# A pooled-attention and token-mixing kernel on one core: the written issue order drawn up anew, with each weight block's signs right behind its absolute values

## The chip, the cores and the metric

The kernel runs on one core of one Trainium2 chip. The time is device time in microseconds (us). It was taken three times for the kernel before: 647.41, 647.52 and 649.43, median 647.52. A core has TensorE (PE in the rows, its weight loads are PEld), VectorE (DVE), ScalarE (ACT) and GpSimd (POOL), which compute, and SyncE (SP), which here issues nearly all DMA transfers. Each engine takes its own instructions strictly in the order in which the program issues them.

## The reference

Inputs are q, k, v of 8 batches, 8 heads, 576 tokens and 64 channels, and four weight matrices. The weights arrive as 64-bit floats.

```
k_p, v_p = mean of k, v over groups of 8 tokens          # 72 keys per head
attn     = softmax(q @ k_p.T / sqrt(64)); sum gets +1e-9 # per head, 576 x 72
x        = attn @ v_p, heads side by side                # 8 x 576 x 512
theta    = x @ w_theta                                   # 512 x 512
zr, zi   = x * cos(theta), x * sin(theta)
y        = w_tok_r @ zr + w_tok_i @ zi                   # contraction over tokens, 576 x 576 each
u        = x + y
out      = u + max(u @ w_ch, 0)                          # 512 x 512
```

## The kernel before

The work is cut into named streams, each a Python generator whose every step issues a few instructions. A stream's name tells its batch and its part: k (load keys), K (pool them, turn them into `kpT`), Q (load and turn queries), v and V (the same for values), S (softmax of one tile of 128 tokens), E (turn the attention by 16 small DMAs, batches 2 to 7 only), X (attention times values, one pair of heads, into `xT`), T (rotate: theta, sine, cosine, z of one tile), Z (split a quarter of z in two parts, zh and zl), M (mix: the token contraction for one quarter of the channels and one part of the tokens), F (final: w_ch, relu, output). Without a batch: h0 to h3 (w_theta by 128 rows), w0.0 to w4.0 (the token matrices by 128 rows, .0 real and .1 imaginary), W0 to W4 (their transposition on PE), c0 to c3 (w_ch).

Products that need more than PE's short format are done in three matmuls: each operand is split in a high part (a cast) and a low part (the rest), which is what the names ending in h and l are. M has 27 matmuls for each of its 64 pieces: zh with WTh, zh with WTl, zl with WTh (the order is reversed for the second token part).

What sets the order is a table, the string `SCHEDULE` at line 30: 1834 words, each the name of a stream. A word issues that stream's next step. A last letter v, g or a tells the engine of a step that has a choice: DVE, POOL or ACT. The loop at the end of `tile_attn_moe` reads it:

```
for word in SCHEDULE.split():
    name, engine = (word[:-1], word[-1]) if word[-1] in "vga" else (word, None)
    now[0] = engine
    next(streams[name])
```

There is no other planner: semaphores between engines follow from the data. A buffer's next user waits until its last one is done.

The steps that the prediction speaks of, by line:

- `to_f32` makes 32-bit floats of 64-bit ones, for each block of h, w and c. Its five steps: the absolute value of the high words on ACT (L289), the sign bits of the same words on ACT, written as 16-bit halves of a block that is otherwise zero (L293), both joined on DVE (L300), the power of two on DVE (L302), the low words times that power on DVE (L304). Only the two ACT steps are free of each other. The sign blocks are two buffers, `chh_st` and `chl_st`, used in turn.
- `token_weights` (L345) loads a w block and calls `to_f32`; `turn_weights` (L373) transposes it on PE (L377, L380) and splits it (L172 high part, L388 low part).
- `load` (L441 to L456) loads keys and values; `pool_on_pe` (L497, L499) sums groups of 8 on PE for batch 0; `keys` (L508, L518) transposes the sums. The second half of the keys of batch 0, k0.1, goes into the buffer `early`. For batch 1 the groups are summed by `pool_sum` (L423, L428) on DVE or POOL.
- `soften`: scores on PE (L637), their maximum on DVE (L667), the exponentials with their sums on ACT (L672, eight of L675, L691, in batches 0 and 1), the reciprocal (L695) and the products (L714, L721). In batch 0, tiles 1 and 3 use a buffer named `spare`.
- `rotate`: the low part xl (L851), the matmuls for theta (L858, bank pt), rounding on ACT (L862), the difference on DVE (L864), sine and cosine on ACT (L875, L878, L883).
- `take`: zh (L172) and zl (L909). `mix`: py (L923), u (L929), uh (L172), ul (L936). `final`: pf (L952), oT (L958).

```
nc.scalar.activation(t, hi.bitcast(F32), AF.Abs, scale=2.0**-112)      # L289
yield
nc.scalar.activation(sign..., hi.bitcast(F32), AF.Copy, scale=2.0**-60) # L293
yield
nc.vector.scalar_tensor_tensor(ti, ti, 3, sign, ...)                    # L300
```

Of the kernel before, what the change touches and what calls it, by code (L numbers as in the profile page):

```python
# [30 lines left out]
k0.1 k0.0 Q0.0 w0.0 w0.0 w0.0 K0.0 K0.0a K0.1 w0.0 k0.2 h0 Q0.4 h0 h0 h0 K0.1a K0 Q0.0 Q0.0v h0 h1 h1 K0.2 K0.2v  # L31
Q0.1 h0 h1 h1 h0 h1 K0a K0 K0v S0.0 S0.0 h2 h2 h2 h2 h0v h0 Q0.4 Q0.4v Q0.1 Q0.1a Q0.3 Q0.3 Q0.3v S0.1 S0.0 S0.0
S0.0 S0.1 S0.1 S0.1 S0.1 Q0.2 Q0.2 h1 Q0.2v S0.2 S0.0 S0.0v S0.0g w0.1 w1.0 w0.1 w0.1 w1.0 h2 h2 k1.0 w0.0 w0.0
S0.2 S0.2 S0.2 S0.2 w0.1 K1.0v S0.1 w1.0 w1.0 v0.0 S0.3 S0.3 S0.3 S0.0 w1.0 w1.0 S0.1g S0.1v v0.1 V0.0 V0.1 V0v
S0.3 v0.2 V0.2 S0.4 S0.2 V0 S0.4 S0.1 S0.0v S0.1a S0.0 S0.0a h1 h1v h1 k1.1 K1.1g w1.1 h2 h3 h3 h3 h3 w0.1 h3 h3
w0.1 S0.1 S0.1a S0.2g S0.2g S0.2 S0.2a X0.0.0 X0.0.0a K1 S0.3 S0.3 S0.3g S0.2 S0.2v X0.0.1 X0.0.1v S0.4 S0.4
S0.4 w1.1 h2a Q1.0 h3 Q1.0 h3a X0.0.3 S0.3g S0.3 S0.3a S0.3 S0.4 S0.4g S0.3v k1.2 K1.2g X0.0.3v W0 W0a S0.4g
X0.0.2 K1v h2 X0.0.2v T0.0g T0.0g S0.4 W0 S0.4a S0.4 S0.4a X0.2.2 X0.2.2a w2.1 T0.1a w2.0 w2.0 W0 W0a w2.1 h3
w1.1 w1.1 v1.0 V1.0v w1.1 w1.1 W0 T0.0 T0.0 X0.2.0 X0.2.0a T0.0 T0.0 T0.0 W1 v1.2 W1a X0.2.1 X0.2.1a T0.0a T0.0
X0.2.3 w4.0 w2.1 w2.1 w3.0 w2.0 w2.0 w2.0 w2.1 w2.0 T0.1v T0.1 X0.2.3a X0.2.3a T0.2g w2.1 T0.1 W1 W1 T0.0 K1  # L40
T0.0 W1v W1 T0.4a w3.0 w3.0 T0.1 T0.1 T0.1 T0.1a K1v Q1.1 Q1.1 W2 W2a w3.0 w3.0 w3.0 W2 w3.1 T0.2g T0.2 T0.4g
T0.1 T0.2 T0.2 T0.2 T0.2 T0.2a T0.2 T0.1 T0.3g T0.3g T0.3 T0.2 T0.1 T0.3 T0.2 T0.3 W2 W2a W2 T0.4 w3.1 w3.1 w3.1
w3.1 w3.1 w4.0 w4.0 w4.0 w4.0 W3 T0.3 T0.3 T0.4 T0.4 T0.4 W3a T0.4 v1.1 V1.1g V1g c0 W3 T0.3a T0.3 T0.3 T0.3 c0
c0 w4.0 W3 W3a W3 T0.4 T0.4 Z0.0a V1.2g c0 c0 c0 Z0.0v W4 c0v W4a W4 W4a W4 W4v W4 Z0.1a Z0.1v W4a W4 k2.2 K2.2v
M0.0.0 M0.0.0 c0g c0g c1 c1 c1 c1 c1 c1 c1v c1v c1v M0.0.1 Z0.2g S1.0 c2 c2 M0.0.0v M0.0.0g c2 M0.0.1 M0.0.1g
S1.0 S1.0 Z0.2v M0.1.0 M0.1.0 c2 c2 c2 c2v c2g M0.2.0 V1g M0.2.0 M0.2.0a M0.2.0g S1.0 M0.1.0a S1.0v S1.0v c2v V1
V1g c3 c3 c3 M0.1.1 Z0.3v M0.1.1 M0.1.1a M0.1.1g S1.0 S1.0a S1.1 S1.1 S1.1 S1.0 S1.0 S1.0v S1.0 S1.1 S1.1v
M0.2.1 M0.2.1 Z0.3g S1.1g M0.3.0 c3 c3 V1v M0.2.1a M0.2.1v S1.1 c3 c3g c3g c3g S1.2 S1.2 S1.2 S1.1v S1.1 S1.1
M0.3.0 S1.2 Q2.0 S1.1a M0.3.0g M0.3.0g S1.1 M0.3.1 M0.3.1 S1.3 S1.3 X1.0.0 X1.0.0v S1.2g S1.2g M0.3.1v M0.0.1v
v2.2 M0.1.0g k2.0 K2.0g S1.3 F0.0.0 F0.0.0 F0.0.0 X1.0.1 X1.0.1a M0.3.1v F0.0.1 F0.0.1 F0.0.1 S1.4 S1.4 X1.0.2  # L50
X1.0.2v Q2.0 S1.3 F0.1.0 F0.1.0 X1.0.3 X1.0.3a T1.0g T1.1a S1.2 S1.2a S1.2 S1.2 S1.2a S1.2 F0.1.1 F0.1.1 S1.3g
S1.3g F0.0.1 S1.3 S1.3v k2.1 S1.3 S1.3 S1.3v S1.3 F0.1.0 F0.1.1 T1.0g K2.1g T1.0 S1.4 S1.4 T1.0 T1.0 T1.0 T1.0
T1.0a T1.0 F0.2.1 F0.2.1 S1.4g S1.4g S1.4 S1.4v S1.4 S1.4 S1.4v S1.4 T1.0 T1.0 T1.1g T1.1 X1.2.0 X1.2.0a Q2.1
Q2.1 K2 K2a V2.2g v2.0 k3.2 X1.2.1 T1.1 T1.1 K2 K2a S2.0 S2.0 X1.2.1a V2.0g X1.2.2 X1.2.2a X1.2.3 X1.2.3v T1.2v
T1.2v v2.1 V2.1g T1.3g T1.3g T1.1 T1.1 T1.1a F0.1.1 T1.1 T1.1 S2.0 T1.1 S2.0 S2.0g T1.2 T1.2 T1.2 F0.2.0 F0.2.0
F0.2.0 K3.2g S2.1 S2.1 F0.2.1 T1.2 T1.2 T1.2a T1.2 T1.2 T1.2 k3.0 K3.0g T1.3 S2.1 T1.3 S2.0 S2.1 T1.3 T1.3 Q3.0
X1.2.3a S2.2 T1.4a T1.4g S2.1v S2.1 F0.2.1 S2.2 T1.3 T1.3a T1.3 F0.3.0 S2.2 T1.3 T1.3 T1.4 T1.4 S2.2 T1.4 T1.4
T1.4 T1.4 S2.2v V2g V2g V2 k3.1 K3.1g S2.3 S2.3 T1.4 K3 Z1.0g F0.3.1 V2g V2g F0.3.0 F0.3.0 S2.4 K3a F0.3.1
F0.3.1 Z1.0v M1.0.0 Q3.0 Z1.1a Z1.1v E2.0 S2.2 E2.0a E2.0a M1.0.0 E2.0g E2.0v S2.3 S2.3 S2.3v K3 K3a M1.0.1
M1.0.1 Z1.2a v3.0 V3.0g X2.0.0 X2.0.0v M1.1.0 M1.1.0 S2.3 X2.0.2 X2.0.2a M1.0.0v Z1.2g M1.1.0g Q3.1 M1.2.0 S2.4  # L60
S2.4 M1.1.0g Q3.1 S2.4 S2.4v S2.4 X2.0.1 X2.0.1a M1.2.0 M1.2.0v M1.2.0v v3.1 M1.1.1 M1.1.1 M1.1.1v X2.0.3 V3.1g
v3.2 X2.0.3v T2.0a V3.2g T2.1a S3.0 S3.0 S3.0 k4.0 K4.0g S3.0 Z1.3g M1.0.1g S3.0v T2.0v M1.2.1 M1.2.1 M1.2.1g
Z1.3v M1.1.1g S3.1 M1.0.1g T2.0 S3.1 S3.1 S3.1 M1.3.0 M1.3.0 E2.2 S3.0 E2.2a F0.3.1 E2.2g E2.2g E2.2v T2.0 T2.0
M1.3.1 M1.3.1 M1.3.1a M1.3.1v M1.3.0g M1.3.0g S3.1v M1.2.1g S3.1 X2.2.0 X2.2.0a S3.2 S3.2 X2.2.1 T2.0 T2.0
X2.2.1a T2.0a T2.0 T2.0 T2.0 F1.0.1 X2.2.2 F1.0.1 T2.1v X2.2.2a M1.0.0g F1.0.0 F1.0.0 F1.0.1 k4.1 K4.1g F1.0.0
S3.2 X2.2.3 S3.2 S3.2v X2.2.3a Q4.0 T2.2g X2.2.3a T2.1 F1.0.1 T2.1 T2.1 F1.1.1 S3.3 S3.3 T2.1 T2.1 T2.1a T2.1
T2.1 v4.0 T2.1 V3g V3g T2.2g V3 T2.2 T2.2 T2.2 T2.2 T2.2 F1.1.0 k4.2 T2.2v T2.2 T2.2 T2.3g T2.2 T2.3g T2.3 S3.4
F1.1.1 F1.1.0 F1.1.0 F1.1.1 T2.3 T2.3 V4.0g T2.3 T2.3 T2.3v K4 T2.3 T2.3 T2.3 Q4.0 V3v T2.4g T2.4g K4.2g T2.4
T2.4 T2.4 E3.0 T2.4 E3.0a S3.2 K4a F1.2.0 F1.2.0 T2.4 T2.4 F1.1.1 T2.4 F1.2.1 F1.2.1 E3.0g F1.2.0 F1.2.1 Z2.0a
K4 V3g F1.3.1 F1.3.1 F1.3.0 F1.3.0 Z2.0v Z2.1a Z2.1v E3.0g E3.0g X3.0.0 X3.0.0a S3.3 S3.3 v4.1 V4.1g S3.3g S3.3  # L70
M2.0.0 M2.0.0 Q4.1 M2.0.0g M2.0.0g F1.2.1 S3.4 Q4.1 v4.2 V4.2g S3.4 S3.4 S3.4g X3.0.1 M2.0.1 M2.0.1 S3.4 k5.2
K5.2g M2.1.0 M2.1.0 X3.0.1a X3.0.2 X3.0.2a K4a S4.0 S4.0 S4.0 F1.3.1 F1.3.0 X3.0.3 Z2.2a Z2.2v M2.0.1a M2.0.1g
M2.1.1 M2.1.1 M2.1.1g M2.1.1g X3.0.3a T3.0v T3.0v Z2.3a M2.2.0 M2.1.0g M2.1.0g M2.2.0 M2.2.0a Z2.3v M2.3.0 k5.0
K5.0v M2.3.0 M2.3.0a S4.0 S4.0v E3.2 S4.0 E3.2v E3.2g E3.2g E3.2g M2.2.1 M2.2.1 S4.1 S4.1 S4.1 S4.1 S4.1v M2.3.1
M2.3.1 M2.3.1a M2.3.1v k5.1 K5.1g F1.3.1 S4.2 S4.2 v5.0 T3.0 T3.0 X3.2.0 T3.0 T3.0 X3.2.0a S4.2 M2.2.0g M2.2.1g
M2.2.1v M2.3.0g F2.0.0 S4.1 Q5.0 X3.2.1 X3.2.1v T3.0 T3.0a F2.0.0 F2.0.0 T3.1a T3.1g F2.0.1 F2.0.1 F2.0.1 X3.2.2
X3.2.2a S4.2 S4.2g S4.3 S4.3 X3.2.3 V4g X3.2.3a X3.2.3g T3.1 F2.0.1 S4.4 T3.0 T3.0 T3.0 V4v V4 V4g V4v S4.3
T3.2v T3.2g T3.1 T3.1 F2.1.0 T3.3g S4.3 F2.1.0 F2.1.0 Q5.0 T3.1 T3.1 T3.1a T3.1 T3.3g T3.1 F2.1.1 F2.1.1 T3.1
F2.1.1 E4.0 T3.2 T3.2 T3.2 F2.2.1 F2.2.1 T3.2 T3.2 T3.2v T3.2 T3.2 T3.2 S4.2 T3.3 S4.3v F2.1.1 T3.3 T3.3 K5 K5a
S4.4 T3.3 T3.3 T3.3a T3.3 T3.3 T3.3 F2.2.0 F2.2.0 F2.2.0 F2.2.1 Q5.1 F2.2.1 T3.4g T3.4g T3.4 T3.4 T3.4 T3.4 T3.4  # L80
T3.4 E4.0g Q5.1 T3.4 F2.3.1 F2.3.1 E4.0g E4.0g E4.0g X4.0.0 F2.3.0 K5 K5a F2.3.0 S5.0 V5.0g X4.0.0a S4.3 X4.0.1
X4.0.1a F2.3.0 F2.3.1 Z3.0g Z3.0v M3.0.0 Z3.1v Z3.1v M3.0.0 S4.4 S4.4 S4.4v S4.4 X4.0.2 X4.0.2a M3.0.1 X4.0.3
X4.0.3a M3.0.0a M3.0.1 M3.0.1a M3.0.1g Z3.2a v5.1 V5.1v M3.1.0 T4.1g T4.1v T4.0v T4.0v M3.1.0 M3.1.0a S5.0
M3.1.0g Z3.2v S5.0 S5.0 S5.0v M3.1.1 M3.1.1 M3.2.0 M3.2.0 M3.2.0g Z3.3a Z3.3v M3.3.0 Q6.0 E4.2 E4.2a E4.2v E4.2v
M3.3.0 M3.3.0v E4.2g M3.3.0g S5.1 S5.1 M3.2.1 S5.1 S5.1 X4.2.2 X4.2.2a M3.2.1 M3.2.1v T4.0 S5.0 M3.0.0g X4.2.0
M3.2.0g k6.0 K6.0g F2.3.1 F3.0.0 F3.0.0 F3.0.0 T4.0 T4.0 X4.2.0a v5.2 V5.2g S5.1g S5.1 X4.2.1 X4.2.1a M3.3.1
M3.1.1g M3.1.1v T4.0 T4.0 T4.0v T4.0 k6.1 K6.1g M3.3.1 M3.3.1a T4.0 T4.0 X4.2.3 M3.2.1g X4.2.3v X4.2.3g V5v V5v
V5 V5v V5v M3.3.1g T4.1 T4.1 T4.1 T4.1 T4.1 T4.1a T4.1 T4.1 T4.1 v6.0 T4.2g S5.2 S5.2 F3.0.1 F3.0.1 E5.0 T4.2g
T4.2 F3.1.0 T4.4a T4.2 T4.2 T4.3a T4.3v S5.3 S5.2 S5.2 S5.2g F3.2.0 F3.1.0 F3.0.1 F3.0.1 S5.3 T4.2 T4.2 T4.2a
T4.2 E5.0g E5.0a T4.2 T4.2 T4.3 T4.3 T4.3 F3.1.1 F3.1.0 F3.1.1 F3.1.1 F3.1.1 S5.4 T4.3 F3.2.0 T4.3 T4.3a T4.3  # L90
T4.3 T4.3 T4.4g S5.2 T4.4 T4.4 T4.4 T4.4 T4.4 k6.2 T4.4 T4.4 E5.0g E5.0g F3.2.1 F3.2.1 F3.2.0 F3.2.1 F3.3.1
F3.3.1 V6.0g Z4.0g Z4.0g F3.3.0 F3.3.0 v6.1 S5.3 S5.3 K6.2g V6.1g F3.2.1 Q6.0 F3.3.1 F3.3.0 X5.0.0 X5.0.0v
M4.0.0 M4.0.0 Z4.1a Z4.1g S5.3v S5.3 M4.0.1 X5.0.1 X5.0.1v M4.0.1 M4.1.0 M4.0.0g M4.0.1v M4.0.1g S5.4 S5.4
# [1003 lines left out]
```

## Time and profile before

| what | value |
|---|---|
| three timed runs | 647.41, 647.52, 649.43 us |
| the profiled execution, by its own clock | 646.99 us |
| its span, first to last instruction | 645.1 us |
| mean granted TensorE clock | 0.973 of full speed |
| PE busy | 603.7 us, 94% of the span |
| first scores (L637) | at 16.76 us |
| first theta matmul (L858) | at 57.07 us |
| first mixing matmul (L923) | at 100.2 us |

Positions are us from the start of the span. The profiled execution took 1.89 us more than its span, and is 0.53 under the median of the three runs. "Waits" are times in which an engine had an instruction that could not start; what ended the wait is named behind the arrow. A granted clock of 1.00 is the upper of TensorE's two levels (2.4 GHz); a mean below that mixes the two levels, the lower being 1.2 GHz.

### The profile page before, as it was taken

What the parts mean: (1) busy time and instruction counts of PE and PEld (TensorE: products, weight loads), DVE (VectorE), ACT (ScalarE), POOL (GpSimd) and SP (SyncE); (2) the same over time, 40 slices, a digit from 0 to 9 for tenths busy, and PEclk for the clock granted to TensorE, in tenths of its full rate; (3) what the DMA queues carried; (4) which work ended last, traced back from release to release, by engine and by line L of the source; (5) the groups of instructions that cost most, each with busy time, mean ns of one, the idle gap of its engine ahead of it and who ended that gap; (6) DMA issues with size and microseconds to landing.
All of it is one profiled execution on the core that took longest, in us unless ns stands there. A gap on an engine that the chain in (4) does not pass through costs nothing.

```text
span 645.1 us, 11179 instructions
## 1 busy us (share of the span) xinstructions
PE 603.7 (94%) x4012; PEld 552.0 (86%) x4012; DVE 472.6 (73%) x839; ACT 306.0 (47%) x668; POOL 344.7 (53%) x381
## 2 busy tenths in 40 slices
PE   5878888999879999999999999999999999999996
PEld 4755578987769988999899989998899889999996
DVE  4866589877788877788889877777777787656234
ACT  4847573847872375326542473237522552243010
POOL 2123242557677777675733848774736645451640
PEclk9869698999999999999999999999999999999998
DMA  9859312145764766356566336454252432302204
GB/s 271 217 120 211 83 34 75 35 95 112 134 121 102 123 99 115 78 105 96 88 94 117 76 50 116 95 102 67 45 93 36 81 50 38 60 2 38 38 1 74
DMA packets 239911, 57.83 MB, mean 90 GB/s; under 512 B 227952, under 2 KB 228464, under 8 KB 239856
## 3 DMA queue, kind: packets, MB, share of 16 engines
q1 hardware_dynamic: 239856, 57.12, 45.6%
q8 instruction: 32, 0.52, 0.4%
q14 instruction: 23, 0.19, 0.1%
HBM read 37.81 MB, written 9.44 MB: 73 GB/s over the span
## 4 chain that ended last, share of the span: by engine, by line
PE 60%; DVE 13%; ACT 10%; DMA 5%; POOL 4%; SPq 4%; issue 3%; DVEq 0%; ACTq 0%; POOLq 0%
PE py L923 27%; PE pf L952 10%; PE pt L858 9%; PE pv L835 5%; PE s L637 4%; SPq L788 3%; ACT e L675 2%; DMA kpst<-in_k_dram 2%; DMA vpst<-in_v_dram 1%; PE px L868 1%; DMA wraw<-in_moe_w_tok_r_dram 1%; DVE g L864 1%; ACT g L862 1%; DVE zl L909 1%; PE ths L331 1%
## 5 line engine op out<-in xcount | busy, mean ns | idle before, releaser
L923 PE MATMUL py<-WTl,zh 128*128 128x256 f32 (+1 forms) x576 | 87.3, 296 | 0.0
L923 PE MATMUL py<-WTh,zh 128*128 128x256 f32 (+1 forms) x576 | 87.1, 299 | 0.3 <-ACT zh L172 0.2
L923 PE MATMUL py<-WTh,zl 128*128 128x256 f32 (+1 forms) x576 | 84.5, 294 | 0.0
L923 PEld LDWEIGHTS py<-WTh,zh 128*128 128x128 f32 x576 | 81.0, 191 | 1.0 <-issue 0.5
L923 PEld LDWEIGHTS py<-WTl,zh 128*128 128x128 f32 x576 | 80.4, 190 | 0.1
L923 PEld LDWEIGHTS py<-WTh,zl 128*128 128x128 f32 x576 | 77.4, 188 | 0.2
L936 POOL TENSOR_TENSOR ul<-xT,uh 128x256 fp32r<-128x256 f32 (+1 forms) x46 | 41.9, 919 | 30.1 <-ACT uh L172 25.7
L929 DVE TENSOR_TENSOR xT<-py,xT 128x256 f32<-128x256 f32 (+1 forms) x64 | 28.4, 443 | 32.2 <-PE py L923 32.1
L637 PE MATMUL s<-kpT,qT 128*128 128x144 f32 (+1 forms) x320 | 49.9, 301 | 2.1 <-DVE ri L695 1.8
L952 PE MATMUL pf<-uh,chh 128*128 128x256 f32 (+1 forms) x256 | 47.1, 306 | 1.5 <-DVE oT L958 1.5
L637 PEld LDWEIGHTS s<-kpT,qT 128*128 128x128 f32 (+1 forms) x320 | 43.4, 188 | 5.1 <-ACT mx L672 2.0
L858 PE MATMUL pt<-th,xh 128*128 128x512 f32 x160 | 46.2, 411 | 1.6 <-DVE g L864 0.8
L851 POOL TENSOR_TENSOR xl<-xT,xh 128x512 fp32r<-128x512 f32 x27 | 36.4, 1348 | 18.6 <-ACT xh L172 15.0
L858 PE MATMUL pt<-th,xl 128*128 128x512 f32 x160 | 43.9, 396 | 1.8 <-DVE xl L851 1.1
L686 ACT ACTIVATE e<-e 128x576 f32<-128x576 f32 (+1 forms) x30 | 20.6, 686 | 51.2 <-DVE e L682 51.0
L952 PE MATMUL pf<-ul,chh 128*128 128x256 f32 (+1 forms) x256 | 44.5, 296 | 0.0
L952 PE MATMUL pf<-uh,chl 128*128 128x256 f32 (+1 forms) x256 | 44.4, 296 | 0.0
L858 PE MATMUL pt<-tl,xh 128*128 128x512 f32 x160 | 43.9, 397 | 0.0
L862 ACT ACTIVATE g<-pt,c_magic 128x512 f32<-128x512 f32 x38 | 26.1, 687 | 35.8 <-PE pt L858 30.4
L952 PEld LDWEIGHTS pf<-uh,chh 128*128 128x128 f32 x256 | 37.4, 189 | 3.3 <-DVE oT L958 2.2
L864 DVE SCALAR_TENSOR_TENSOR g<-g,pt 128x512 f32<-128x512 f32 x38 | 25.8, 679 | 19.4 <-ACT g L862 19.3
L858 PEld LDWEIGHTS pt<-th,xl 128*128 128x128 f32 x160 | 29.7, 188 | 10.1 <-DVE xl L851 2.3
(241 smaller groups left out, 1426.7 us busy)
## 6 DMA issues: line engine op xcount, KB each, us to landing
qsst<-in_q_dram SPq DMA_DIRECT2D x112, 72.0 KB, 3.1
out_dram<-R SPq DMA_DIRECT2D x112, 72.0 KB, 2.1
kpst<-in_k_dram SPq DMA_DIRECT2D x15, 512.0 KB, 4.1
vpst<-in_v_dram SPq DMA_DIRECT2D x28, 256.0 KB, 4.2
eraw<-G SPq DMA_DIRECT2D x96, 60.0 KB, 2.3
eraw<-G SPq DMA_DIRECT2D x96, 40.0 KB, 2.1
WTh_st<-in_moe_w_theta_dram SPq DMA_DIRECT2D x4, 512.0 KB, 7.6
wcraw<-in_moe_w_ch_dram SPq DMA_DIRECT2D x4, 512.0 KB, 3.3
```

What stands on the lines that cost most here:

```text
L637: nc.tensor.matmul(scs[c // 2][:n, 2 * SP * (c % 2) : 2 * SP * (c % 2 + 1)], qT[:, c, t0 : t0 + n], kpT[:, c, :], start=True, stop=True,)
L686: nc.scalar.activation(e[:n], e[:n], AF.Exp, scale=scale)
L788: nc.sync.dma_start(blocks(Ex, jj, i), blocks(Gx, i, jj))
L835: nc.tensor.matmul(pv[:, :gn], l, r, start=i == 0, stop=i == len(terms) - 1)
L851: ENG[pick()].tensor_tensor(xl, xT[:, :, o], f32(xh), ALU.subtract)
L858: nc.tensor.matmul(pt, l[:, c, :], r[:, c, :], start=i == 0, stop=i == 11)
L862: nc.scalar.activation(g, pt, AF.Identity, bias=c_magic)
L864: nc.vector.scalar_tensor_tensor(g, g, MAGIC, pt, ALU.subtract, ALU.subtract)
L923: nc.tensor.matmul(py[:, :n], l[:, kk, :], r[:, kk, t], start=i == 0, stop=i == 3 * NK - 1)
L929: nc.vector.tensor_tensor(u, py[:, :n], u, ALU.add)
L936: ENG[pick()].tensor_tensor(ul[:, c, t], u, f32(uh[:, c, t]), ALU.subtract)
L952: nc.tensor.matmul(pv[:, :n], l[:, kk, o], uhl[r][:, kk, t], start=i == 0, stop=i == 11)
```

## The change

Only the string `SCHEDULE` is another. Both tables hold 1834 words, the same steps of the same streams in another sequence, and a stream's own steps keep their order. Of the words that name an engine, 261 named POOL, 181 DVE and 175 ACT; now it is 231, 204 and 182. By the program, DVE gets 27 instructions more (868 for 841), POOL 24 fewer (362 for 386), ACT 5 fewer, of which 2 are loads of function tables; PE (3786) and SP (525) have as many as before. The low parts zl (L909) go from 12 on POOL and 20 on DVE to 22 and 10; the low parts ul (L936) from 46 and 18 to 36 and 28. In the new table the sign step of a block (L293) stands directly behind the absolute value (L289) of the same block. From batch 1 on the sequence of PE's work is nearly the old one, and the last words, those of batch 7's M and F, are the same.

The diff, cut to the first line of the table on either side:

```
 SCHEDULE = """
-k0.1 k0.0 Q0.0 w0.0 w0.0 w0.0 K0.0 K0.0a K0.1 w0.0 k0.2 h0 Q0.4 h0 h0 h0 K0.1a K0 Q0.0 Q0.0v h0 h1 h1 K0.2 K0.2v
...
+k0.0 w0.0 k0.2 K0.0 K0.2 h0 h1 w0.0 w0.0 w0.0 h0 h0 h0 h0 h0 h1 h1 h1 h1 h1 K0.0v K0.2v h0 h2 h2 h2 h0a h0 h2 h2
...
```

Three places of it, as the instructions stand on their engines. The first is ACT around the first theta tile of batch 0 (T0.0, `g_0`). `wsrc_a<-wraw_...` is an absolute value, `chl_st` or `chh_st<-wraw_...` a sign; the first number behind `wraw` is the half (0 real, 1 imaginary), the second only tells blocks apart. Before:

```order
L289 ACTIVATE wsrc_a<-wraw_1_547 128x576
L293 ACTIVATE chl_st<-wraw_1_401 128x576
L862 ACTIVATE g_0_587<-pt_0_574,c_magic 128x512
L172 COPY xT_427<-pv_256_0_589 128x320
L875 ACT_TABLE_LOAD
L875 ACTIVATE sn_0_599<-g_0_587 128x512
L172 CAST WTh<-wt_0_602 128x8x128
L172 COPY xT_427<-pv_256_1_622 128x320
L878 ACTIVATE g_0_587<-g_0_587 128x512
L883 ACTIVATE g_0_587<-g_0_587,c_cos 128x512
L293 ACTIVATE chl_st<-wraw_1_547 128x576
```

After:

```order
L289 ACTIVATE wsrc_a<-wraw_1_537 128x576
L293 ACTIVATE chl_st<-wraw_1_537 128x576
L289 ACTIVATE wsrc_a<-wraw_0_546 128x576
L293 ACTIVATE chh_st<-wraw_0_546 128x576
L172 COPY xT_394<-pv_256_2_552 128x320
L862 ACTIVATE g_0_569<-pt_0_556,c_magic 128x512
L172 CAST WTh<-wt_8_572 128x128
L289 ACTIVATE wsrc_a<-wraw_1_583 128x576
L293 ACTIVATE chl_st<-wraw_1_583 128x576
```

Before, nine instructions stand between the absolute value of block 547 and its sign, among them ones that need PE (pv, wt) and the rotation's own sine and cosine. Now none stands between.

The second place is ACT at the softmax of tiles 2 and 3 of batch 0 (`s_2`, `s_3`). Before:

```order
L289 ACTIVATE wsrc_a<-wraw_0_272 128x576
L672 ACTIVATE mx_2_283<-mx_2_283 128x8
L675 ACTIVATE e_2_284,sm_2_286<-s_2_259,mx_2_283 128x72 x8
L691 ACTIVATE sm_2_286<-sm_2_286,c_eps 128x8
L293 ACTIVATE chh_st<-wraw_0_272 128x576
L672 ACTIVATE mx_3_314<-mx_3_314 128x8
```

After:

```order
L691 ACTIVATE sm_1_246<-sm_1_246,c_eps 128x8
L672 ACTIVATE mx_2_274<-mx_2_274 128x8
L675 ACTIVATE e_2_275,sm_2_277<-s_2_264,mx_2_274 128x72 x8
L691 ACTIVATE sm_2_277<-sm_2_277,c_eps 128x8
L672 ACTIVATE mx_3_318<-mx_3_318 128x8
L675 ACTIVATE spare,sm_3_321<-s_3_0_310,mx_3_318 128x72 x4
```

The weight block that was begun ahead of tile 2 and ended behind it is gone from here; tiles 1, 2 and 3 follow each other.

The third place is SP at the start, the transfers in the order of issue. `early<-in_k_dram` is k0.1, `kpst` k0.0, `qsst` the first queries, `kprst` k0.2. Before:

```order
L441 DMA early<-in_k_dram 128x2x512
L441 DMA kpst_0_107<-in_k_dram 128x2x512
L551 DMA qsst_0_110<-in_q_dram 128x8x64
L360 DMA wraw_0_112<-in_moe_w_tok_r_dram 128x1152
L453 DMA kprst_139<-in_k_dram 64x512
L309 DMA WTh_st<-in_moe_w_theta_dram 128x1024
```

After:

```order
L441 DMA kpst_0_106<-in_k_dram 128x2x512
L360 DMA wraw_0_108<-in_moe_w_tok_r_dram 128x1152
L453 DMA kprst_110<-in_k_dram 64x512
L309 DMA WTh_st<-in_moe_w_theta_dram 128x1024 x3
L441 DMA early<-in_k_dram 128x2x512
L551 DMA qsst_0_186<-in_q_dram 128x8x64
```

k0.1 was first and is now seventh, behind k0.0, one block of token weights, k0.2 and three blocks of w_theta; the first queries come behind it.

## Rows read from the trace of the kernel before

**Rows 1.** Page, part 1: busy us (share of the span) xinstructions

```profile
PE 603.7 (94%) x4012; PEld 552.0 (86%) x4012; DVE 472.6 (73%) x839; ACT 306.0 (47%) x668; POOL 344.7 (53%) x381
```

**Rows 2.** Windows: stretch, length, busy PE PEld DVE ACT POOL, PEclk, DMA, GB/s

```profile
0.00:57.07 57.07, 41.72 (x240) 32.26 (x241) 37.69 (x73) 33.91 (x126) 16.28 (x27) 0.88 0.78 207
57.07:100.20 43.13, 35.28 (x159) 25.25 (x158) 30.93 (x50) 28.95 (x47) 10.97 (x14) 0.83 0.36 79
100.20:188.50 88.30, 80.24 (x539) 72.86 (x539) 72.24 (x143) 57.35 (x169) 51.88 (x63) 0.99 0.46 95
188.50:598.20 409.70, 405.10 (x2767) 380.47 (x2768) 316.21 (x544) 183.86 (x325) 248.39 (x262) 1.00 0.45 79
```

**Rows 3.** Waits of PE, 0 to 100.2 us: us in total, times, longest

```profile
PE wt L377 <- DVE WTl L388: 5.8, 5, 1.8
PE vpp L499 <- DVE Ve L174: 5.3, 1, 5.3
```

**Rows 4.** Waits of DVE, 57.07 to 100.2 us

```profile
DVE wsrc_a L300 <- ACT chl_st L293: 10.7, 3, 6.7
DVE g L864 <- ACT g L862: 1.1, 1, 1.1
```

**Rows 5.** Timeline of DVE from 57 us: start, us, operation, [idle before <-releaser]

```profile
60.07 0.76 DVE L300 SCALAR_TENSOR_TENSOR wsrc_a<-wsrc_a,chl_st 128x576 int32<-128x576 int32 x1 [3.36 <-ACT chl_st L293]
...
63.49 0.68 DVE L864 SCALAR_TENSOR_TENSOR g<-g,pt 128x512 f32<-128x512 f32 x1
...
70.88 0.76 DVE L300 SCALAR_TENSOR_TENSOR wsrc_a<-wsrc_a,chl_st 128x576 int32<-128x576 int32 x1 [6.71 <-ACT chl_st L293]
```

**Rows 6.** Timeline of ACT, 57 to 80 us

```profile
58.57 0.72 ACT L289 ACTIVATE wsrc_a<-wraw 128x576 f32<-128x576 f32 x1
...
70.02 0.83 ACT L293 ACTIVATE chl_st<-wraw 128x576 f16<-128x576 f32 x1
...
77.17 0.69 ACT L862 ACTIVATE spare<-pt,c_magic 128x512 f32<-128x512 f32 x1 [4.92 <-PE pt L858]
```

**Rows 7.** Timeline of DVE, 26 to 37 us

```profile
26.11 0.76 DVE L304 SCALAR_TENSOR_TENSOR wsrc_b<-wraw,wpow 128x576 fp32r<-128x576 uint32 x1
...
31.80 0.76 DVE L300 SCALAR_TENSOR_TENSOR wsrc_a<-wsrc_a,chh_st 128x576 int32<-128x576 int32 x1 [2.10 <-ACT chh_st L293]
...
33.69 1.71 DVE L304 SCALAR_TENSOR_TENSOR wsrc_b<-wraw,wpow 128x576 fp32r<-128x576 uint32 x1
```

**Rows 8.** Timeline of ACT, 27 to 37 us

```profile
30.93 0.83 ACT L293 ACTIVATE chh_st<-wraw 128x576 f16<-128x576 f32 x1
...
36.18 0.32 ACT L675 ACTIVATE spare<-s,mx 128x72 f32<-128x72 f32 x1 [2.65 <-DVE spare L721]
```

**Rows 9.** Timeline of PE, 5 to 18 us

```profile
6.34 3.75 PE L497 MATMUL kpp<-kpst,ident 128*128 128x128 f32 x16 [6.34 <-DMA kpst<-in_k_dram]
10.86 2.05 PE L497 MATMUL kpp<-early,ident 128*128 128x128 f32 x16 [0.76 <-ACT kp L172]
...
16.76 1.25 PE L637 MATMUL s<-kpT,qT 128*128 128x144 f32 x8
```

**Rows 10.** Windows, columns as in rows 2: 5 to 10 us

```profile
5.00:10.00 5.00, 3.66 (x16) 3.49 (x16) 0.54 (x9) 0.75 (x2) 0.00 (x0) 1.00 1.07 318
```

**Rows 11.** Groups of L909: count, busy us, mean ns of one, idle before

```profile
L909 POOL TENSOR_TENSOR zl<-z,zh 128x1152 fp32r<-128x1152 f32 x12 | 33.3, 2775 | 0.6
L909 DVE TENSOR_TENSOR zl<-z,zh 128x1152 fp32r<-128x1152 f32 x20 | 29.7, 1489 | 1.4 <-ACT zh L172 1.4
```

**Rows 12.** L923 up to 262 us: ns min/median/max, first and last start

```profile
L923 PE MATMUL py<-WTh,zl x11: 276/276/313, 260.3 to 262.0; 128*128 128x256 f32 x9, 128*128 128x320 f32 x2
L923 PE MATMUL py<-WTh,zh x9: 278/282/283, 258.2 to 259.1; 128*128 128x256 f32 x9
```

**Rows 13.** Waits of PE, 188.5 to 645 us

```profile
PE pf L952 <- DVE oT L958: 1.5, 3, 0.7
```

**Rows 14.** Timeline of POOL, 23 to 45 us

```profile
33.52 2.45 POOL L423 TENSOR_TENSOR kpst<-kpst 128x512 f32<-128x512 f32 x2 [2.63 <-DMA kpst<-in_k_dram]
```

## What the rows say the new order does to the time

> **What bounds the kernel now.** I read the busy shares first. PE has 603.7 of 645.1 us [rows 1], no other engine over 73%: PE is the bound on the whole, so a new order can only give back PE's idle time and its stretches at the lower clock. Where these lie is told by the windows [rows 2]: from 188.5 to 598.2 us PE is busy for 405.10 of 409.70 us at clock 1.00. Nothing is to be had there. From 0 to 57.07 us, the first theta matmul, it is busy for 41.72; from there to 100.2, the first mixing matmul, for 35.28 of 43.13, and at 0.83. The head is where the order decides.
>
> Who decides inside the head is read from the waits. From 57.07 to 100.2 DVE is busy for 30.93 us and waits for 10.7 us, in three pieces, for a sign on ACT, and for 1.1 us for the rounding [rows 2, 4]: 42.7 of the 43.13 us are told by DVE alone. DVE is what ends this stretch, though PE is busy longer. The timeline shows the mechanism: DVE joins value and sign (L300) and stands still for 6.71 us until the sign is there at 70.88 [rows 5]. On ACT the absolute value of a block was begun at 58.57, its sign only at 70.02 [rows 6], since copies out of PE, a table load and the sine's steps stand between (the first place of the change). ACT itself was not full: 28.95 of 43.13 us [rows 2]. PE's largest wait on DVE in the head, 5.8 us for WTl in five pieces [rows 3], is the same chain further on: a weight block that is late on DVE is late at its split.
>
> From 0 to 57.07 us the same thing is smaller: one sign wait of 2.10 us at 31.80, because the sign stands behind tile 2's eight exponentials on ACT [rows 7, 8], and then ACT waits for 2.65 us for DVE before tile 3's exponentials at 36.18 [rows 8]. PE waits once for 5.3 us for Ve, another DVE step [rows 3].
>
> **The change, part by part.** The sum is made against the profiled execution, 646.99 us (span 645.1 and 1.89 around it), 0.53 under the median of the runs. Nothing is added or removed but engine choices, so I go by stretches.
>
> A, theta to mixing, 43.13 us. Every sign now follows its absolute value. The three sign waits, 10.7 us, lose their cause: a sign takes 0.83 us and an absolute value 0.72 [rows 6], and the sign buffer is free as soon as DVE has joined the block before. What is late next? DVE's own work and its rounding wait, 30.93 + 1.1 = 32.0 us; ACT's work is 28.95; PE's 35.28 us at 0.83 would be 35.28 × 0.83 = 29.3 at the upper clock [rows 2, 4]. The least is so 32.0, or −11.1. It won't be reached: ACT also stood for 4.92 us for theta's second tile from PE [rows 6], and that wait is no sign's. I put 3.0 of it, some 60%, on the path: 32.0 + 3.0 = 35.0, or −8.1. The other end: with the sign wait gone DVE reaches steps that wait for PE in turn, and only the one short stall of 3.36 less the time of a block (0.72 + 0.83) goes, 3.36 − 1.55, near −2. I take −8, between −11 and −2.
>
> B, start to theta, 57.07 us. Gains: the sign's 0.83 on ACT, DVE's 2.10 behind it and ACT's 2.65 behind that DVE step leave the softmax of tiles 1 to 3, 5.6 together [rows 7, 8]; of PE's 5.3 for Ve I count a quarter, 1.3, since it overlaps with the same stall [rows 3]. A loss: k0.1, the second half of batch 0's keys, was first in the queue and is seventh (the third place of the change). By their shapes the queue up to its end now holds k0.0 (0.52 MB), a weight block (0.59), k0.2 (0.13), three blocks of w_theta (1.57) and itself (0.52), 3.34 MB; before, both key halves were first, 1.05 MB, and the first pooling began at 6.34 us, when they had landed [rows 9]. The extra 2.29 MB at 318 GB/s [rows 10] are 7.2 us, so its pooling starts at 13.5 instead of 10.86. From that pooling to the first scores it was 16.76 − 10.86 = 5.9 us [rows 9]; 13.5 + 5.9 = 19.4, or +2.7 at most where nothing in the 5.9 is drawn ahead; none where the w_theta work that now runs before it was in the way. B is 2.7 − 5.6 − 1.3 = −4.2. I take −4. Ends: all of the 5.3 for Ve gone, 2.7 − 5.6 − 5.3 = −8; the late keys in full and no gain, +3.
>
> C, from the first mixing matmul on. Sequence nearly the same on PE, and PE idles for 4.6 us in 410 [rows 2], with no wait above 1.5 in all [rows 13]. What changes are engines: ten more zl on POOL, at 2.775 us instead of 1.489 on DVE [rows 11]. The cover is the 18 matmuls that come before zl's first: their start at 258.2, zl's at 260.3, so 2.1 us [rows 12]. If zl were begun no sooner than its first matmul's chain, POOL's would end 0.7 late, ten times 0.7 or +7 at the worst. The twelve that are on POOL today make no row among PE's waits [rows 13], so I take 0; and between 100.2 and 188.5 PE is idle for 8.1 us [rows 2], of which 2 might come back. Ends −2 and +7.
>
> Sum: −8 − 4 + 0 = −12; 646.99 − 12 = 635.0 us.
>
> One row speaks against the engine choices. L304, with two inputs in SBUF, took 1.71 us at 33.69 beside a POOL addition that began at 33.52, and 0.76 alone at 26.11 [rows 7, 14]. The Trainium skill, "SBUF — State Buffer", section "Who interferes with whom", says that a DVE instruction with two SBUF inputs and a GpSimd one that reads SBUF shut each other out for a whole instruction; by that rule, the trace agrees here, with 0.95 us more.
>
> **The rivals.**
>
> 1. Half the gain. The sign waits go, but the next late thing is PE's and ACT's own exchange: ACT's 4.92 us for theta counts in full and PE's 7.85 idle us at 0.83 stay mostly [rows 2, 6]. A gives −4 instead of −8 and B −1: 642. For it: 35.28 us of PE work at the granted clock leave only 7.85 us to win. Against: part of the low clock is itself due to PE's idling.
>
> 2. DVE and POOL get in each other's way. Each of ten more zl on POOL and ten ul moved to DVE finds one neighbour of the sort of L304, 0.95 us each [rows 7, 14]; where a third of 20 falls on the path, 6 us are lost of 12: 641. For it: the 1.71. Against: with 248 us of POOL and 316 of DVE in 409.7 they overlap all the time already, and PE still has its 4.6 idle us [rows 2].
>
> 3. No change, 647 ± 1.9: the wait moves from the sign to what the sign had been placed behind. For it: each copy and sine that a sign now stands ahead of lets PE or the rotation go on, and is later by the sign's 0.83. Against: 14.18 us of ACT idle in A, 43.13 − 28.95 [rows 2], into which 0.83 fits.
>
> 4. Slower. k0.1 and with it the first queries land late; this one delay decides where it holds back more than it does on paper. Every tile of batch 0 needs all the keys, so the whole softmax starts later. If the queue moves at the mean of the head, 207 GB/s [rows 2], the 2.29 MB are 11.1 us: pooling at 17.4, scores at 23.3, +6.6. Against B's gain of 1.3 + 5.6 this is nothing lost; but where A also gives no more than its −2 and the softmax gains stay hidden behind the late keys, it is 646.99 + 6.6 − 2 = 651.6, and with a smaller delay 649. It decides from scores later than about 22 us, with theta's first matmul after 60. For it: the first 10 us moved at 318 GB/s with a DMA share of 1.07, so the queue is full [rows 10]. Against: PE's first pooling was itself waiting for both halves.
>
> **How the numbers follow.** Forecast 635 with 0.52; rival 1 with 0.16, rival 2 with 0.06; no change 0.10; slower 0.16. A measurement of this kernel tells apart about 0.3%, 1.9 us. Faster: 0.52 + 0.16 + 0.06 = 0.74; same 0.10; slower 0.16. The likeliest case alone has 626 to 640: 626 is −11 in A, −8 in B and −2 in C, the least of all three, 640 is the sum with A at −3. The range goes from 626 to 649, which takes in rivals 1 to 3 and the smaller form of rival 4.
>
> **What would show it.** In the changed kernel's waits of DVE before the first mixing matmul the sign rows should be under 2 us together (10.7 now). The first scores should come at 18 to 20 us, the first theta matmul at about 53, the first mixing matmul at about 88, and from there to the end the distance should be what it is now, 645.1 − 100.2 = 544.9, within 2. The forecast is wrong in A if a wait of the same size stands under another name on DVE, in B if the first theta matmul is later than 57, in C if PE waits for zl (L909) or ul (L936) by more than 2 us.

## The result, and the profile after

The changed kernel took 641.13 us, the kernel before 647.81 on the same chips (medians of 12 runs each). The ratio is 0.9898, with a 95% interval of 0.9869 to 0.9927: 6.6 us faster, by 4.7 to 8.5. The forecast was 635.0 in a range of 626 to 649. The way and the range held; the gain is a little over half of the 12 us.

The profiled execution took 641.1 us, its span is 639.4. The windows, with the columns of [rows 2], are cut at the first theta matmul (53.37 us; before 57.07) and at the first mixing matmul (85.55; before 100.21):

```profile
0.00:53.37 53.37, 40.88 (x239) 30.85 (x239) 34.65 (x68) 35.48 (x130) 15.59 (x24) 0.90 0.84 224
53.37:85.55 32.18, 28.08 (x158) 21.47 (x158) 29.21 (x46) 28.19 (x46) 15.04 (x19) 1.00 0.40 97
85.55:173.00 87.45, 81.43 (x535) 74.59 (x534) 74.64 (x147) 58.03 (x168) 48.69 (x55) 0.96 0.44 94
173.00:195.00 22.00, 18.68 (x128) 17.82 (x126) 18.16 (x30) 11.03 (x22) 9.10 (x11) 0.92 0.56 90
195.00:598.00 403.00, 395.46 (x2695) 371.07 (x2695) 310.49 (x550) 170.60 (x295) 240.28 (x242) 1.00 0.43 77
```

The second line answers the 43.13 us of [rows 2]: 32.18 us, with as many PE instructions (158, 159 before), almost as much work on DVE, and the clock at 1.00 instead of 0.83. PE's busy time fell from 35.28 to 28.08 us for the same work, since the clock rose with it. The runs below show that it goes with the signs: in this stretch it is 0.96 where only the signs are early, and 0.91 where they are late again in the changed order. The waits of DVE in this stretch, for [rows 4]:

```profile
DVE WTl L388 <- ACT WTh L172: 1.0, 2, 0.5
DVE z L887 <- ACT g L883: 0.6, 1, 0.6
DVE wsrc_a L300 <- ACT chh_st L293: 0.6, 2, 0.3
```

10.7 us for signs became 0.6. By the first mixing matmul the changed kernel is 100.21 − 85.55 = 14.7 us ahead. At the end it is 645.1 − 639.4 = 5.7 ahead. From there on it takes 639.4 − 85.55 = 553.85 us, where the kernel before took 544.89. So 9 us were given back in a part whose order I had called nearly the same. Cut at the first mixing matmul of batches 0, 1 and 2 (called M0, M1, M2 from here on; not the stream M), before and after:

```profile
100.21:188.43 88.22, 80.17 (x539) 72.79 (x539) 72.16 (x143) 57.34 (x169) 51.82 (x63) 0.99 0.46 95
188.43:258.18 69.75, 69.41 (x476) 64.93 (x476) 56.95 (x96) 36.62 (x63) 53.94 (x63) 1.00 0.61 113
258.18:645.10 386.92, 377.12 (x2605) 356.77 (x2603) 274.92 (x480) 149.22 (x265) 211.67 (x216) 1.00 0.40 68
```

```profile
85.55:173.97 88.42, 82.40 (x543) 75.36 (x541) 75.58 (x149) 59.00 (x169) 48.69 (x55) 0.96 0.44 94
173.97:249.28 75.31, 70.87 (x477) 66.35 (x474) 62.64 (x106) 38.58 (x68) 41.70 (x52) 0.98 0.51 94
249.28:639.40 390.12, 377.97 (x2606) 357.23 (x2604) 279.81 (x500) 144.88 (x254) 215.19 (x209) 1.00 0.40 70
```

Of the 9 us, 0.2 lie before M1, 5.6 between M1 and M2, 3.2 behind M2. Between M1 and M2 PE is idle for 4.4 us instead of 0.3, and its work takes 1.5 us more. The largest single place shows among PE's waits after 85.5 us:

```profile
PE py L923 <- DVE zl L909: 2.6, 1, 2.6
PE px L868 <- DVE z L887: 2.6, 5, 0.8
PE pv L835 <- ACT xT L172: 2.0, 3, 0.9
PE pv L835 <- DVE eraw L809: 1.8, 3, 0.8
PE pt L858 <- POOL xl L851: 1.5, 1, 1.5
```

Before, no row of PE's waits after the first mixing matmul named zl; the largest from 188.5 us on was 1.5 us for oT [rows 13]. The timelines of POOL, DVE and PE around it:

```profile
182.61 3.00 POOL L909 TENSOR_TENSOR zl<-z,zh 128x1152 fp32r<-128x1152 f32 x1 [3.30 <-ACT zh L172]
```

```profile
182.34 3.55 DVE L423 TENSOR_TENSOR vpst<-vpst 128x512 f32<-128x512 f32 x2
185.93 0.29 DVE L428 TENSOR_TENSOR vp<-vpst 128x128 f32<-128x128 f32 x1
186.13 1.35 DVE L909 TENSOR_TENSOR zl<-z,zh 128x1152 fp32r<-128x1152 f32 x1
```

```profile
183.67 1.24 PE L923 MATMUL py<-WTl,zh 128*128 128x256 f32 x9
187.54 1.74 PE L923 MATMUL py<-WTh,zl 128*128 128x256 f32 x9 [2.63 <-DVE zl L909]
```

Read them together. POOL works on zl of the third quarter from 182.61 to 185.6. DVE's two additions, which end at 185.9, take 3.55 us (1.15 in a run below). Behind them on DVE stands zl of the second quarter, and PE needs that one first: it stands still for 2.63 us. The nine matmuls that follow take 1.74 us, nine such before the wait 1.24: behind the wait the granted clock is 0.59 for 4 us.

```profile
187.50:191.70 4.20, 4.16 (x20) 4.16 (x21) 3.77 (x8) 0.88 (x3) 0.34 (x1) 0.59 1.13 192
```

The Trainium skill, "SBUF — State Buffer", section "Who interferes with whom", says that a DVE instruction with two SBUF inputs contends with a GpSimd instruction that reads SBUF, and calls the ports that they share "an exclusive lock"; these rows agree, with 2.40 us more for the two additions.

A second place of the kind, on DVE and then on POOL, at 413 us:

```profile
413.18 3.28 DVE L701 TENSOR_TENSOR en<-e,ri 128x576 f32<-128x576 f32 x1
```

```profile
413.14 2.70 POOL L909 TENSOR_TENSOR zl<-z,zh 128x1152 fp32r<-128x1152 f32 x1
```

The same instruction took 0.75 us at 402.67 in this trace (on 64 partitions) and 0.76 at 189.15 (on 128). PE waits for 0.85 us there, at 415.90, but for this zl itself and not for DVE; the two runs below that mend the place too take 0.2 and 0.9 us less behind M2.

### The profile page after: what moved, and what is told of

Its sections match the earlier page's. It is cut to its first block, busy times and chain, and to the rows that moved or that the text cites. A ratio compares the mean times of both kernels' runs of the same rounds, so it can differ in the third digit from the quotient of the medians.

```text
span 639.4 us, 11172 instructions
## 1 busy us (share of the span) xinstructions
PE 600.2 (94%) x4012; PEld 551.3 (86%) x4012; DVE 481.9 (75%) x866; ACT 306.1 (48%) x663; POOL 336.2 (53%) x357
## 4 chain that ended last, share of the span: by engine, by line
PE 58%; DVE 14%; SPq 8%; ACT 6%; DMA 5%; POOL 5%; issue 3%; DVEq 0%; POOLq 0%; ACTq 0%
PE py L923 19%; PE pt L858 12%; PE pf L952 12%; SPq L788 7%; PE pv L835 5%; PE s L637 4%; PE px L868 2%; DMA eraw<-G 2%; DMA kpst<-in_k_dram 2%; DMA vpst<-in_v_dram 1%; DVE eraw L809 1%; POOL vpst L423 1%; DMA WTh_st<-in_moe_w_theta_dram 1%; POOL zl L909 1%; DVE mx L667 1%
## 5 line engine op out<-in xcount | busy, mean ns | idle before, releaser
L923 PE MATMUL py<-WTh,zl 128*128 128x256 f32 (+1 forms) x576 | 86.1, 297 | 3.7 <-DVE zl L909 2.6
L923 PE MATMUL py<-WTl,zh 128*128 128x256 f32 (+1 forms) x576 | 88.1, 298 | 0.0
L923 PE MATMUL py<-WTh,zh 128*128 128x256 f32 (+1 forms) x576 | 87.2, 299 | 0.0
L923 PEld LDWEIGHTS py<-WTh,zl 128*128 128x128 f32 x576 | 78.7, 191 | 4.4 <-DVE zl L909 2.8
L923 PEld LDWEIGHTS py<-WTh,zh 128*128 128x128 f32 x576 | 80.8, 190 | 0.5 <-issue 0.2
L923 PEld LDWEIGHTS py<-WTl,zh 128*128 128x128 f32 x576 | 81.2, 192 | 0.0
L909 POOL TENSOR_TENSOR zl<-z,zh 128x1152 fp32r<-128x1152 f32 x22 | 61.2, 2787 | 25.0 <-ACT zh L172 19.9
L851 POOL TENSOR_TENSOR xl<-xT,xh 128x512 fp32r<-128x512 f32 x29 | 38.7, 1334 | 31.1 <-DVE xh L174 15.4
L936 POOL TENSOR_TENSOR ul<-xT,uh 128x320 fp32r<-128x320 f32 (+1 forms) x36 | 32.0, 898 | 27.7 <-DVE uh L174 15.7
L172 ACT CAST uh<-xT 128x256 fp32r<-128x256 f32 (+1 forms) x27 | 11.3, 427 | 62.1 <-DVE xT L929 62.0
L686 ACT ACTIVATE e<-e 128x576 f32<-128x576 f32 (+1 forms) x30 | 20.6, 686 | 38.2 <-DVE e L682 35.0
```

What stands on the lines that cost most here:

```text
L686: nc.scalar.activation(e[:n], e[:n], AF.Exp, scale=scale)
L851: ENG[pick()].tensor_tensor(xl, xT[:, :, o], f32(xh), ALU.subtract)
L909: ENG[pick()].tensor_tensor(zl, z[:, :, o], f32(zh), ALU.subtract)
L923: nc.tensor.matmul(py[:, :n], l[:, kk, :], r[:, kk, t], start=i == 0, stop=i == 3 * NK - 1)
L936: ENG[pick()].tensor_tensor(ul[:, c, t], u, f32(uh[:, c, t]), ALU.subtract)
```

## The experiments

Each ratio is against the kernel before on the same chip, with its 95% interval. In the first four runs the table stood on five lines fewer, so their lines are lower by 5 (L295 there is L300). "Head" is the time to the first mixing matmul, "rest" the span less the head. The last three columns cut the rest at M1 and M2.

| kernel | us | ratio | first theta | head | rest | M0 to M1 | M1 to M2 | M2 to end |
|---|---|---|---|---|---|---|---|---|
| before | 647.81 | 1 | 57.07 | 100.21 | 544.89 | 88.2 | 69.8 | 386.9 |
| changed | 641.13 | 0.9898 (0.9869 to 0.9927) | 53.37 | 85.55 | 553.85 | 88.4 | 75.3 | 390.1 |
| e1_signs | 632.16 | 0.9752 (0.9713 to 0.9791) | 51.35 | 84.21 | 543.59 | 86.7 | 69.7 | 387.1 |
| e2_new_head | 634.77 | 0.9799 (0.9761 to 0.9837) | 49.95 | 82.83 | 549.37 | 92.6 | 69.8 | 386.9 |
| e2_old_head | 657.86 | 1.0138 (1.0100 to 1.0175) | 58.77 | 101.65 | 554.65 | 91.3 | 71.6 | 391.7 |
| e3_zl | 639.02 | 0.9865 (0.9830 to 0.9901) | 53.69 | 85.89 | 550.81 | 88.3 | 72.7 | 389.7 |
| e4_keys | 649.07 | 1.0034 (1.0005 to 1.0062) | 61.29 | 94.18 | 553.52 | 88.4 | 74.9 | 390.3 |
| e5_zl2 | 642.04 | 0.9922 (0.9893 to 0.9952) | 53.65 | 85.87 | 554.63 | 88.8 | 76.6 | 389.2 |
| e6_late | 655.16 | 1.0122 (1.0089 to 1.0155) | 61.59 | 99.10 | 554.30 | 88.3 | 75.7 | 390.4 |
| e7_best | 634.24 | 0.9794 (0.9768 to 0.9821) | 55.27 | 89.56 | 545.44 | 88.5 | 70.2 | 386.8 |
| e8_zl3 | 638.45 | 0.9850 (0.9827 to 0.9873) | 53.39 | 85.67 | 550.93 | 88.8 | 72.2 | 389.9 |
| e9_letters | 659.47 | 1.0182 (1.0156 to 1.0207) | 53.22 | 86.07 | 569.43 | 88.2 | 79.7 | 401.6 |
| e10_later_signs | 638.83 | 0.9840 (0.9812 to 0.9868) | 55.48 | 88.35 | 543.95 | 87.4 | 69.7 | 386.9 |

The rest sorts the kernels by itself. With the later order and letters of before it is 543.6 to 545.4, with heads from 84 to 100 us. With the changed later order it is 553.5 to 554.7, with heads from 86 to 102; only the two runs that mend a place in it (e3_zl, e8_zl3) are shorter. Head and rest don't know of each other. Behind M1 single traces can be compared closely: the five kernels that have the old order there (before, e1_signs, e2_new_head, e7_best, e10_later_signs) agree to about 0.5 us from M1 to M2 and to 0.3 behind M2.

**Signs alone.** The order before, the signs early. One of the moves:

```
 w1.0                                              (absolute value)
+w1.0                                              (sign)
 h2 h2 k1.0 w0.0 w0.0 S0.2 S0.2 S0.2 S0.2 w0.1 K1.0v S0.1
-w1.0                                              (sign)
 w1.0                                              (joined on DVE)
```

> The order before, in which only the signs of five weight blocks (w1.0, w1.1, w2.0, w2.1, w4.0) are issued directly behind their absolute values, or, for w2.1, as soon as its sign buffer is free. Theory 1, the signs are the cause of the gain in the head: DVE's 10.7 us of waits for signs between the first theta matmul and the first mixing matmul fall under 2, the first mixing matmul comes 6 to 11 us earlier than 100.2, and the time is 637 to 642. Theory 2, the signs are only one of several late things and the new order as a whole is the cause: the waits move to PE's results, the first mixing matmul comes less than 4 us earlier, the time is 644 to 648.

632.16 us, faster than either theory said and faster than the changed kernel; the two intervals don't touch. (w4.0's sign stood in its place already, so four signs moved.) Its windows, up to the first theta and the first mixing matmul and to the end:

```profile
0.00:51.35 51.35, 39.87 (x240) 31.05 (x241) 36.56 (x74) 34.31 (x127) 16.20 (x27) 0.93 0.85 230
51.35:84.21 32.86, 28.72 (x159) 22.26 (x158) 29.48 (x50) 27.71 (x45) 10.80 (x14) 0.96 0.47 103
84.21:627.80 543.59, 526.80 (x3617) 495.30 (x3615) 402.09 (x717) 243.14 (x497) 316.33 (x340) 0.99 0.44 78
```

Four moved steps do all that the new order does for the head, 16.0 us, and the rest stays. Theory 1 is right in kind and low in size.

**The signs one by one.** As the run above, with w1.0's sign left behind tile 2's exponentials.

> The order before with the signs of w1.1, w2.0, w2.1 and w4.0 early, and that of w1.0 left behind tile 2's exponentials. Theory 1, the gain of the five signs (16 to 17 us) is two separate gains, some 6 of w1.0 in the softmax and some 10 of the later ones between theta and mixing: 10 to 11 us won here, 636 to 638, with the position at 20 us of PE work unchanged from before. Theory 2, the later ones give less by themselves because the weights of w1.0 come late: 640 to 644.

638.83 us, 0.8 over what was said; by the ratio −10.4 us of 648.42 (before, on that chip). The stretch from theta to mixing is 88.35 − 55.48 = 32.87, as with all four signs (32.86), so the three later signs are worth 10.3 us there, and w1.0's sign 55.48 − 51.35 = 4.1 us ahead of it, in this pair of executions. They are two separate gains. The 4.1 is the rougher one: first theta is 1.6 us earlier than before here with the same words in front of it, and 53.22 and 55.27 in two other executions with the words of e1_signs (last section). The timed runs are firmer: 0.9840 against 0.9752 is 5.7 us for the whole kernel, and the intervals don't touch.

**Signs late in the changed order.** Sign and join of w1.0 behind S0.2's sum (L691), and the signs of w2.0 (with what follows of that block) and w2.1 behind T0.0's sine and cosine:

```
 w1.0
-w1.0 w1.0
 ... S0.2 S0.2 S0.2 S0.2
+w1.0 w1.0
```

> The changed kernel with two places undone: sign and join (L293, L300) of w1.0 behind tile 2's exponentials, and sign of w2.0 and w2.1 (and what follows of w2.0) behind T0.0's sine and cosine steps on ACT, as in the order before. All else is the changed order. Theory 1, the place of the signs is what the head gains by: 6 to 12 us of 14 are lost again, 647 to 653, and DVE's waits for signs before the first mixing matmul are over 5 us. Theory 2, it is the new order as a whole, which has other work ready for DVE: under 3 us lost, 641 to 644.

655.16 us: 14 us lost, a little more than theory 1 said, and nearly all of it in the head (99.10 for 85.55; the rest is 554.30 for 553.85). DVE's waits up to 100 us:

```profile
DVE wsrc_a L300 <- ACT chh_st L293: 12.5, 4, 5.0
DVE mx L667 <- PE s L637: 6.8, 5, 3.4
```

Done in the old order and undone in the new one, the place of the signs moves the head by about the whole gain. Theory 2 falls. Behind M0 this run repeats the changed kernel stretch by stretch (88.3, 75.7, 390.4), though it gets there 13.6 us later: what is lost there is not the price of an early head.

**Which half gives back.** First the changed order up to the first final piece (F0.0.0), then that of before; second the old one up to the first mixing matmul, then the changed one.

```
 words of the changed table up to F0.0.0
+words of the table before that are left, in its order, with its letters
```

> The changed order up to the first piece of the final stage of batch 0 (about 122 us), then the order and the engine letters of before. Theory 1, the changed kernel gives back 8 of its 14 us because of pieces in its own later order (zl and its neighbours on POOL and DVE): here the 14 us stay, 632 to 636. Theory 2, what is early in the head runs into something that doesn't move with it (transfers, the clock), whatever the later order: 639 to 643, as the changed kernel.

> The order before up to the first mixing matmul, then the changed order and its letters. Theory 1 (the changed order's later part is slower by 8 us): 652 to 657. Theory 2 (only an early head is given back): 645 to 649.

634.77 and 657.86 us. The old head with the changed rest takes 554.65 for the rest, 9.8 more than before: the loss is in the changed later order, not in being early, and theory 2 (a thing that doesn't move) falls. The joined kernel loses it in other stretches (3.1, 1.9 and 4.8 us, for 0.2, 5.6 and 3.2 in the changed kernel), part of it perhaps at the join: what a piece costs hangs on what it meets. The new head keeps most of its lead but not all: its rest is 549.37, 4.5 over before's. The trace tells where. From M0 to the first final piece, the changed order's part, it takes 36.62 us (36.54 in the changed kernel, 37.06 before); from there to M1, just behind the place where the tables are joined, 55.96 (51.87 and 51.15); from M1 on it is before's to 0.1 us. So the 4.5 us are the join's own, and neither table's.

**The zl near 185.** One letter:

```
-Z1.2g
+Z1.2v
```

> The changed kernel with one letter different: zl of batch 1's third quarter (zl1_2) on DVE instead of POOL. Theory 1: POOL's zl at 182.6 held DVE's two additions (3.55 us for 1.1), DVE's zl1_1 came 2.4 us late, PE stood 2.6 us and then ran at the lower clock until 191.7. Here the additions take 1.1 to 1.3 us, PE's wait is under 1 us, no low clock between 183 and 195, and 4 to 5 us are won: 636 to 637. Theory 2, that the zl on DVE now queues ahead of other things on DVE, or that the low clock comes anyway: under 2 us won, 639 to 641.

639.02 us, at the near end of theory 2's range, and the interval overlaps the changed kernel's. In the trace the rest is 3.0 shorter, 2.6 of it between M1 and M2 (72.70 for 75.31). DVE and PE there:

```profile
182.65 1.15 DVE L418 TENSOR_TENSOR vpst<-vpst 128x512 f32<-128x512 f32 x2 [0.40 <-DMA vpst<-in_v_dram]
184.04 2.62 DVE L904 TENSOR_TENSOR zl<-z,zh 128x1152 fp32r<-128x1152 f32 x2
```

```profile
186.72 1.32 PE L918 MATMUL py<-WTh,zl 128*128 128x256 f32 x9 [1.76 <-DVE zl L904]
```

The additions take 1.15 us as soon as POOL does no zl beside them, and the nine matmuls 1.32; from 173 to 195 the granted clock is 1.00, where it was 0.92. That was the mutual exclusion, shown. But PE still waits 1.76 us. The moved zl now stands on DVE ahead of the one that PE needs, so that the two take 2.62 us in a row, and both stand behind the additions, which wait for a transfer. Of the 2.40 us that the exclusion had cost, 1.3 went into the moved zl itself.

**The order there too, twice.** First zl1_1 directly behind its zh, and zl4_3 on DVE as well:

```
-Z1.2g   +Z1.2v      -Z4.3g   +Z4.3v
 Z1.1a
+Z1.1v
 Z1.2a S2.3 E2.0v E2.0v ...
-Z1.1v
```

> The changed kernel with three steps different: zl1_2 on DVE (as in the run before), zl1_1 issued on DVE directly behind its zh, ahead of the additions for the values that wait for a transfer, and zl4_3 on DVE instead of POOL. Theory 1, these are the two places where the changed kernel gives time back (5 us near 185, 3 us between 401 and 425): PE's wait for zl near 185 is under 0.5 us, DVE's L701 near 413 takes 0.8 us instead of 3.3, and the time is 633 to 636. Theory 2, each repair puts something else late on DVE, which is over 70% busy: 638 to 641.

642.04 us, nothing won: a miss of mine in the edit. PE needs the attention's low part first, and that now stood behind zl:

```profile
185.59 0.58 PE L835 MATMUL pv<-eraw,Vh 128*128 128x256 f32 x1 [3.34 <-DVE eraw L809]
```

Then zl1_1 between that low part and the additions:

```
 E2.0v                (L809)
+Z1.1v
 V2g X2.0.0 X2.0.0a V3.0v ...
-Z1.1v
```

> The changed kernel with three steps different: zl1_2 and zl4_3 on DVE instead of POOL, and zl1_1 on DVE between the attention's low part (L809, which PE waits for first) and the additions for the values that wait for a transfer. In the attempt before, zl1_1 stood ahead of L809 and PE waited 3.3 us for L809 instead. Theory 1, the two places are mended by order and engine alone: PE's waits near 185 are under 1 us together, 5 to 7 us won, 634 to 636. Theory 2, the loss only moves on: 638 to 642.

638.45 us. PE's wait for zl is gone, 0.81 us for the low part is left:

```profile
182.89 0.39 PE L835 MATMUL pv<-eraw,Vh 128*128 128x256 f32 x1 [0.81 <-DVE eraw L809]
183.11 0.28 PE L835 MATMUL pv<-er,Vr 96*128 96x256 f32 x1
183.23 1.23 PE L923 MATMUL py<-WTh,zh 128*128 128x256 f32 x9
184.30 1.24 PE L923 MATMUL py<-WTl,zh 128*128 128x256 f32 x9
185.38 1.19 PE L923 MATMUL py<-WTh,zl 128*128 128x256 f32 x9
```

The place is mended, yet the rest is 550.93: 2.9 of 9 us came back, 3.1 of them between M1 and M2. The time lies in theory 2's range, and is not clear of the one-letter run. The second place is mended too, and was worth little: DVE's L701 takes 0.76 us at 412.33 and at 415.67, and from M2 to the end it is 389.9 us for 390.1 (389.2 in the run before). Of the 9 us, 2.4 between M1 and M2 and 3.0 behind M2 are left. PE's waits there are all under 1.2 us, and their cause stays open.

**The letters by themselves.** The early signs in the old order, with the changed kernel's letters for every zl and ul.

> The order before with its five signs early (632.16 earlier), and the engine letters of the changed kernel for all zl (22 on POOL instead of 12) and all ul (36 on POOL instead of 46), the order otherwise untouched. Theory 1, the letters alone cost what the changed kernel gives back (POOL's zl is slower and shuts DVE out): 638 to 642, PE's waits for zl and ul over 4 us. Theory 2, a zl on POOL is covered wherever the order gives it room, and the loss came from the order around single pieces: 631 to 634.

659.47 us: 26 over the early signs alone in the profiled rest (569.43 − 543.59 = 25.8), far beyond both theories. The order is e1_signs' word for word, only letters differ. PE's waits after 85 us:

```profile
PE pv L835 <- POOL eraw L809: 6.7, 2, 6.4
PE py L923 <- POOL zl L909: 3.5, 4, 1.3
PE pv L835 <- POOL Vr L610: 3.2, 1, 3.2
PE py L923 <- DVE zl L909: 2.2, 1, 2.2
```

The worst is not zl itself but what stands behind it on POOL:

```profile
245.56 2.70 POOL L909 TENSOR_TENSOR zl<-z,zh 128x1152 fp32r<-128x1152 f32 x1 [3.64 <-ACT zh L172]
248.33 2.49 POOL L802 TENSOR_TENSOR er<-eraw,er 32x256 fp32r<-32x256 f32 x2
250.90 2.34 POOL L809 TENSOR_TENSOR eraw<-eraw,eh 128x1024 fp32r<-128x1024 f32 x1
```

POOL waited 3.64 us for this zl's zh, with the low part that PE needed queued behind it; PE stood 6.4 us. The letters of a table belong to its order. In their own order the whole rest, letters and order together, cost 9; no run has that order with the old letters, so how the 9 divide between order and letters is not shown.

**Keys first.** The changed order with k0.1 and the first queries at the front, and the first scores issued ahead of w_theta.

```
-k0.0 w0.0 k0.2 K0.0 K0.2 h0 h1 w0.0 w0.0 w0.0 h0 h0 ...
+k0.0 k0.1 Q0.0 w0.0 k0.2 K0.0 K0.2 h0 h1 w0.0 w0.0 w0.0 K0.0v K0.2v K0.1 K0.1a K0 K0a K0 Q0.0 Q0.0a K0v S0.0 S0.0 h0 h0 ...
```

> The changed order, with k0.1 and the first queries loaded second and third, and the pooling, turning and first scores of batch 0 issued ahead of the w_theta blocks, which follow in their changed order. Theory 1, the late keys cost what the changed order's first scores are late (18.9 to 20.7 us against 16.5 to 16.8): first scores at 13 to 15 us, first theta matmul 3 to 5 us earlier than 53.4, time 636 to 638. Theory 2, the w_theta blocks then come late in turn and hold theta, or the softmax is held by other things: first scores early, but the first theta matmul within 1.5 us of 53.4, time 640 to 642.

649.07 us: theory 2, and worse. The first scores came at 18.79 instead of 20.69, and the first theta matmul at 61.29 instead of 53.37. On DVE the work for w_theta now stands between the first scores and the second tile's queries:

```profile
21.04 0.68 DVE L300 SCALAR_TENSOR_TENSOR WTh_st<-WTh_st,chh_st 128x512 int32<-128x512 int32 x1
...
29.38 0.75 DVE L300 SCALAR_TENSOR_TENSOR wsrc_a<-wsrc_a,chh_st 128x576 int32<-128x576 int32 x1
30.04 0.68 DVE L174 COPY qT<-pq 128x512 f32<-128x512 f32 x1
```

The changed start does that work while the keys are still in the queue; for this order the late keys are the smaller price.

**A better version.** The early signs with two more places: batch 3's keys turned behind the next final piece on PE, and two steps of w4.0 on DVE behind W3's second part.

```
-K3 Z1.0g F0.3.1
+Z1.0g F0.3.1 K3
```

> The order before with its five signs early (632.16 in the earlier run), and two more places: the transposition of batch 3's keys behind the next piece of the final stage on PE (a wait of 1.6 us for POOL), and two of DVE's steps for w4.0 behind the second part of W3's transposition (PE waited 1.5 and 1.8 us for WTl there). Theory 1: both waits shrink, 2 to 3 us won, 629 to 630. Theory 2: the next late thing takes their place, 631 to 633.

634.24 us, ratio 0.9794 beside 0.9752, with intervals that overlap: no gain shown, and the rest is 545.44. The early signs alone have the lowest ratio of all that was run, not clear of this one or of e2_new_head.

## Why the prediction was half right

- **A, theta to mixing: right, the size low.** Taken −8 between −11 and −2, measured 32.18 − 43.13 = −10.95. The sign waits fell from 10.7 to 0.6. The 3.0 us that I put on ACT's wait for theta's second tile did not come: I had said that this wait was no sign's, and it fell with the signs, from 4.92 to 1.8 us. The stretch is 0.2 over my floor of 32.0, but that is chance: DVE was busy for 29.21 us of it, not for the 30.93 of the floor.
- **B, start to theta: the size is luck.** Taken −4, measured 53.37 − 57.07 = −3.70. The late half of the keys was pooled from 13.67 us on, as forecast (13.5). The first scores came at 20.69, 0.7 later than the 18 to 20 that I had named, because that pooling took 3.78 us in this execution and 2.05 in the profiled one of before. Both starts come in both forms (last section). Like with like, B is 49.95 − 57.07 = −7.1 or 53.37 − 58.77 = −5.4: the gain was priced low, and the pair that was profiled hid it. (The 318 GB/s that I took for the first 10 us is of 5 to 10 us alone.)
- **C, the rest: the step that failed.** "I take 0", between −2 and +7, measured 553.85 − 544.89 = +9.0. The sum is −3.7 − 10.95 + 9.0 = −5.7, which is the difference of the spans (−5.7). My own sign of this came: PE waited for zl by more than 2 us, 2.63 in one piece. I priced a moved zl by its own duration against the 18 matmuls that cover it. The cover holds: of 22 zl on POOL one makes PE wait, for 0.9 us. What I left out is what a zl does to others: DVE's two-input instructions stand still beside it (2.40 us at 182.34), and whatever is queued behind a late piece is late too. I had the exclusion as rival 2, in the row that took 1.71 us, and spread it evenly instead of looking for the piece on which PE waits next. The other meeting that was looked at, 2.5 us more at 413.18, made no wait of PE's on DVE. The exclusion explains only part: mending the place near 185 gave back 3 of the 9 us, and the cause of the other 6 is open.
- **"Sequence nearly the same on PE"** was no ground for 0. PE's own sequence was nearly the same; what feeds it on DVE and POOL was not, and PE idles 4.6 us in 410 only as long as all of these arrive in time.
- **The rivals.** Rival 1 named nearly the right time, 642, for a wrong reason: the head gave more than forecast, not half. Rival 2 named 641, the time that was measured, with a chance of 0.06; its mechanism is shown at one place, but its sum, a third of 20 meetings on a gain of 12, is not what happened: 14.7 us were won and 9.0 lost. Rival 4 was wrong: the keys were late, as said, and the first scores with them by 3.9 us (1.7 of it by the longer pooling), yet theta came 3.7 us earlier, and putting the keys first lost 8 us at theta (e4_keys). The changed table has one exception to what was said of it: the sign of the fourth w_theta block does not follow its absolute value directly.

## What to carry to other kernels

When a long order is drawn up anew, gains and losses come from different places, and the sum hides both: compare the two traces at the same work, and cut at landmarks, more than one: the loss looked spread until it was cut by batch, and then 5.6 of 9 us lay in one stretch. Then do the smallest edit that should carry the gain; here four steps gave two and a half per cent, and the whole new order one. An operation that moves to another engine is priced by what stands behind it there, and by what can't run beside it, before its own duration.

## What the runs showed of the hardware that was not expected

The same first words don't take the same time, and they come in two forms. The sixteen matmuls that pool the second half of batch 0's keys took 2.05 us in four of the six kernels that begin with the old words, with the first scores at 16.5 to 16.8 us, and 3.8 in the other two (e2_old_head, e7_best), with the scores at 18.8. With the changed words they took 2.05 us in one of six (e2_new_head), with the scores at 18.91, and 3.7 to 3.8 in five, with the scores at 20.6 to 21.0. The long form of either, and the short one:

```profile
11.23 3.75 PE L492 MATMUL kpp<-early,ident 128*128 128x128 f32 x16 [1.15 <-ACT kp L167]
13.67 3.78 PE L497 MATMUL kpp<-early,ident 128*128 128x128 f32 x16 [1.14 <-DVE kpr L174]
13.62 2.05 PE L492 MATMUL kpp<-early,ident 128*128 128x128 f32 x16 [1.62 <-DVE kpr L169]
```

The granted clock shows this only in part: over the long form it reads 0.50 in the changed kernel and 1.00 in e2_old_head. What decides between the forms is not shown. Up to theta the changed kernel had 0.90 granted and reached it at 53.37; the run with the new head, with the same words up to F0.0.0, had 1.00 and reached it at 49.95:

```profile
0.00:49.95 49.95, 37.22 (x239) 27.66 (x239) 34.59 (x68) 35.49 (x130) 15.58 (x24) 1.00 0.92 238
```

PE was busy for 37.22 us here and 40.88 there with the same 239 instructions. That 3.4 us is half of the spread of the twelve runs of each kernel (643.1 to 649.4 before, 637.2 to 644.6 after). So a single profile tells a head's time only to some 3 us, where the medians of several runs tell 2; two heads are best compared in the same form.
